# Attention scores from float16 pairs with measured scales in place of fp32r pairs, one unit in float32 rows, and one shared ring for g

## The chip, the cores and the metric

The kernel runs on one core of one Trainium2 chip. The time is the device time in microseconds of one execution; of the kernel before three executions are shown, with a median of 924.1 us. Five engines work side by side: TensorE (PE, matmuls; PEld its weight loads), VectorE (DVE), ScalarE (ACT), GpSimd (POOL) and SyncE (SP), which issues the DMAs.

## What is computed

Attention with a decay over 4 batches, 8 heads, 576 positions, 64 per head; behind it two dense blocks over the 2304 rows:

```
scores = q @ k.T / sqrt(64)                      # q, k: (4, 8, 576, 64) float32
cum    = cumsum(log(clip(f, 1e-4, 1)), axis=-1)
scores = where(causal, -1e9, scores + cum[:, :, :, None] - cum[:, :, None, :])
attn   = exp(scores - max); attn = attn / (sum(attn) + 1e-9)
x      = (attn @ v) rearranged to (2304, 512)
h      = x @ w_in; x = maximum(0.01 * h, h) @ w_out          # 512 -> 2048 -> 512
g      = x @ w_gate; out = (g * sigmoid(g) * (x @ w_val)) @ w_out2   # 512 -> 1536 -> 512
```

## The kernel before

**Units.** The work of attention and of the first dense block ("MoE" below) is cut into eight units (b, u): batch b, with u=0 for queries 0 to 319 (three tiles of 128, the first half filled) and u=1 for queries 320 to 575 (two tiles). A u=0 tile sees 128, 256 or 320 keys, a u=1 tile 448 or 576 (576 as two halves of 288). Unit (0,0) is `attention_f32`; the others go through `attention`. While one unit's attention runs, the MoE of the unit before it runs too: `along` interleaves them, so (1,0)'s scores lie beside the MoE of (0,1). `moe_h` makes g (hidden values as float16 pairs, in `g_ring`) and `moe_y` reads it into y1 in DRAM. The last part of the kernel, `gate_val` and `out_stage`, does the second dense block from y1.

**Scores.** For b = 0 a head has one float32 tile `xf` of 66 rows: 64 of k and q, and two rows that add the decay (`rd`). One float32 matmul a tile gives the scores. For b > 0 `prep_head` loads k and q doubled over 128 partitions, rounds them to fp32r (`ta`, on ScalarE), copies the rounded q to `tb`, and makes the rests by two subtractions on VectorE. Two matmuls a tile then add up: `tb` (68 rows: rounded q by rest of k, and four decay rows that `decay` left in `cum_dram`) and `ta` (128 rows). The columns of an fp32r matmul are padded to 256. `exps` then calls `exp_of`: a custom VectorE instruction scales the scores by -0.125 out of PSUM, adds the mask and takes the minimum; ScalarE does the exponential with a sum. `probs` splits the result in two float16 halves, a DMA transposes them, and `pv` multiplies with v.

**Staging.** w_gate, w_val and w_out2 come as float64 and are turned into float32 on VectorE, a piece at a time (`place`, in `gv_places`), spread over the units from (1,1) to (3,1); `prep_gv`, beside the MoE of (3,1), loads them back from DRAM and splits them.

**Order.** Every instruction is first recorded as an operation with an estimated cost; `Plan` then orders each engine's queue and SP's by a list schedule with due times, and emits it. Source order sets buffers and dependencies, and the schedule sets the order in each queue. All instructions of a unit stand under one line of the profile (415), so tiles tell them apart: `att_bytes`, `g_bytes`, `moe_bytes`, `wi_bytes`, `wo_bytes`, `stage` and `smalls` are arenas that hold many buffers; `ta` and `tb` are tiles of their own.

Of the kernel before, what the change touches and what calls it, by code (L numbers as in the profile page):

```python
# [447 lines left out]
def body(ctx, tc, qk, v, f, w_in, w_out, w_gate, w_val, w_out2, out):  # L448
# [175 lines left out]

    def decay():
# [34 lines left out]
        nc.behind = scan  # L660
        for u, (q0, nq, _) in enumerate(UNITS):
            col, _, qc, kc = COLS[u]
            for a, c, n in ((0, kc, KEYS[u]), (2, qc, nq)):
                x = csf[:, a:a + 2, col + c:col + c + n]
                nc.scalar.copy(out=x, in_=one[:, :1].unsqueeze(2).to_broadcast(x.shape))
        nc.behind = None
# [3 lines left out]
        nc.vector.memset(fr, 8.0)  # L670
        for u, (q0, nq, _) in enumerate(UNITS):
            col, wd, qc, kc = COLS[u]
            n = KEYS[u]
            ks = slice(col + kc, col + kc + n)
            qs = slice(col + qc, col + qc + nq)
            nc.vector.tensor_scalar(out=cs[:, 2, ks], in0=cum[:, :n], scalar1=-8.0, scalar2=None, op0=ALU.mult)
            nc.vector.scalar_tensor_tensor(out=cs[:, 3, ks], in0=cum[:, :n], scalar=-8.0, in1=csf[:, 2, ks],
                                           op0=ALU.mult, op1=ALU.subtract)
            nc.scalar.activation(out=cs[:, 0, qs], in_=cum[:, q0:q0 + nq], func=AF.Copy, scale=8.0)
            nc.scalar.activation(out=cs[:, 1, qs], in_=csf[:, 3, col + kc + q0:col + kc + n], func=AF.Copy, scale=-1.0)  # L680
        nc.sync.dma_start(cd, csf)
# [786 lines left out]
```

## Time and profile before

| | |
|---|---|
| median of three runs | 924.1 us (920.23 to 924.16) |
| the profiled execution | 925.66 us, of which span of the instructions 923.9 us |
| PE busy | 908.8 us, 98% of the span |
| PE weight loads | 776.7 us, 84% |
| DVE busy | 794.1 us, 86% |
| ACT busy | 676.1 us, 73% |
| POOL busy | 45.4 us, 5% |
| chain of waits that ended last | PE 58% of the span, DVE 7%, DMA 3%, ACT 3% |
| DMA queue of the kernel | 131.2 MB, 53.5% of the 16 engines' span |

Busy times are unions over the span, and matmuls overlap one another, so two starts in a row tell what a matmul costs better than its duration. A stage below is cut where a unit's MoE matmuls end: 132.6 to 187.5 us is (1,0)'s attention with the MoE of (0,1), 187.5 to 254.7 us (1,1) with the MoE of (1,0), 254.7 to 309.7 us (2,0), 309.7 to 380.2 us (2,1), 380.2 to 434.4 us (3,0), 434.4 to 499.7 us (3,1), 499.7 to 542.3 us the MoE of (3,1); then come gate_val and out_stage.

### The profile page before, as it was taken

Reading aid. Unit: us, or ns where it says so; the run is one execution under the profiler, and the core shown is the slowest. Engines: PE = TensorE matmul, PEld = TensorE weight load, DVE = VectorE, ACT = ScalarE, POOL = GpSimd, SP = SyncE. Lnnn points to the kernel's source line nnn. Section 1 sums busy time; section 2 is a strip of 40 time slices with the busy share of each in tenths; the row PEclk is TensorE's granted clock in tenths of the full one; section 3 lists DMA queues with packets and bytes.
Section 4 is the critical chain, followed back from the end, with each engine's and each line's share of the span. In section 5 each row is a group of like instructions: output and inputs, shape, how many; then the busy total and the mean of one; then the engine's idle time right before and its main releaser. Section 6 shows DMA issues by size and latency. Waiting matters only on the chain.

```text
span 923.9 us, 25387 instructions
## 1 busy us (share of the span) xinstructions
PE 908.8 (98%) x10018; PEld 776.7 (84%) x10018; DVE 794.1 (86%) x2078; ACT 676.1 (73%) x1665; POOL 45.4 (5%) x119
## 2 busy tenths in 40 slices
PE   9999999999999999899999999999999999999998
PEld 5666678877688777788778899999999999999997
DVE  7999999988899999799788999986778695968685
ACT  8886689988689887688886878774647474755553
POOL 3410000000000010000000000000000000000000
PEclk9999999999999999999999999999999999999999
DMA  7568985797999999989867452110101000100001
GB/s 229 179 202 217 271 212 115 187 248 172 259 270 259 255 263 229 298 249 254 188 147 191 140 178 96 64 59 20 37 18 31 25 25 25 37 25 2 26 6 42
DMA packets 163431, 132.81 MB, mean 144 GB/s; under 512 B 117432, under 2 KB 130752, under 8 KB 163280
## 3 DMA queue, kind: packets, MB, share of 16 engines
q1 hardware_dynamic: 163312, 131.20, 53.5%
q8 instruction: 78, 1.28, 0.6%
q14 instruction: 41, 0.34, 0.1%
HBM read 79.99 MB, written 22.83 MB: 111 GB/s over the span
## 4 chain that ended last, share of the span: by engine, by line
PE 58%; DVE 7%; DMA 3%; ACT 3%; issue 1%; POOL 0%; SPq 0%; ACTq 0%; DVEq 0%; POOLq 0%
PE bank L415 58%; DVE att_bytes L415 2%; DVE stage L415 1%; DVE wo_bytes L415 1%; ACT att_bytes L415 1%; DMA tb<-out_dram 1%; ACT moe_bytes L415 1%; DMA att_bytes<-att_bytes 1%; DVE smalls L415 1%; DVE wi_bytes L415 1%; DMA att_bytes<-in_qk_dram 1%; DMA gate_val_dram<-wo_bytes 1%; DVE g_bytes L415 1%; DVE tb L415 0%; DVE ta L415 0%
## 5 line engine op out<-in xcount | busy, mean ns | idle before, releaser
L415 PEld LDWEIGHTS <-att_bytes 128*128 128x128 f16 (+1 forms) x4062 | 233.8, 100 | 18.3 <-issue 14.7
L415 PEld LDWEIGHTS <-wi_bytes 128*128 128x128 f16 x2292 | 192.2, 98 | 42.4 <-issue 3.1
L415 PE MATMUL bank<-g_bytes,wo_bytes 128*128 128x256 f16 (+2 forms) x1472 | 209.7, 299 | 0.0
L415 PE MATMUL bank<-moe_bytes,wi_bytes 128*128 128x320 f16 (+1 forms) x1536 | 194.5, 286 | 1.5 <-ACT moe_bytes L415 1.5
L415 ACT ACTIVATE att_bytes<-att_bytes,smalls 128x320 f32<-128x320 f32 (+11 forms) x308 | 173.7, 591 | 30.1 <-DVE smalls L415 25.5
L415 PEld LDWEIGHTS <-wo_bytes 128*128 128x128 f16 x1344 | 128.1, 98 | 33.5 <-issue 1.8
L415 DVE TENSOR_TENSOR wi_bytes<-bank,wi_bytes 128x256 f32<-128x256 f32 x270 | 109.4, 418 | 45.0 <-PE bank L415 43.6
L415 PEld LDWEIGHTS <-g_bytes 128*128 128x128 f16 x1620 | 125.9, 98 | 9.0
L415 ACT ACTIVATE wi_bytes<-wi_bytes,smalls 128x256 f32<-128x256 f32 (+2 forms) x129 | 69.9, 555 | 44.9 <-DVE wi_bytes L415 42.4
L415 PE MATMUL bank<-wi_bytes,att_bytes 128*128 128x128 f16 x1680 | 98.7, 219 | 0.5 <-ACT wi_bytes L415 0.3
L415 DVE SCALAR_TENSOR_TENSOR att_bytes<-att_bytes,smalls 128x576 f16<-128x576 f32 (+5 forms) x148 | 86.8, 614 | 4.1 <-ACT att_bytes L415 3.7
L415 PE MATMUL bank<-stage,att_bytes 128*128 128x128 f16 (+1 forms) x1389 | 86.7, 221 | 0.6 <-DVE wi_bytes L415 0.6
L415 ACT COPY wi_bytes<-bank 128x256 f32<-128x256 f32 x108 | 38.4, 363 | 51.8 <-PE bank L415 47.6
L415 DVE CUSTOM_DVE_ANT_0 att_bytes<-bank,att_bytes 128x320 f32<-128x320 f32 (+5 forms) x160 | 67.7, 441 | 7.2 <-PE bank L415 7.1
L415 POOL PARTITION_ALL_REDUCE smalls<-smalls x54 | 28.2, 523 | 757.1 <-DVE smalls L415 718.3
L415 PE MATMUL bank<-att_bytes 128*64 128x256 f16 (+4 forms) x828 | 55.5, 262 | 5.5 <-DMA att_bytes<-att_bytes 5.2
L415 ACT ACTIVATE wi_bytes<-wo_bytes 128x256 bf16<-128x256 f32 x108 | 44.0, 410 | 19.2 <-DVE wo_bytes L415 19.2
L415 PE MATMUL bank<-wo_bytes,g_bytes 128*128 128x256 f16 x432 | 55.0, 273 | 0.0
L415 DVE TENSOR_TENSOR g_bytes<-moe_bytes,g_bytes 128x320 f16<-128x320 f32 (+1 forms) x80 | 44.6, 564 | 8.2 <-ACT g_bytes L415 7.8
L415 PE MATMUL bank<-tb 68*128 68x256 f32 (+3 forms) x144 | 49.9, 360 | 1.7 <-ACT att_bytes L415 1.1
L415 DVE SCALAR_TENSOR_TENSOR stage<-stage 128x512 int32<-128x512 int32 x68 | 46.5, 684 | 0.2
L415 DVE SCALAR_TENSOR_TENSOR wo_bytes<-wi_bytes,smalls 128x512 f32<-128x512 f32 x54 | 40.1, 743 | 6.3 <-ACT wi_bytes L415 6.3
(123 smaller groups left out, 1380.1 us busy)
## 6 DMA issues: line engine op xcount, KB each, us to landing
stage<-in_moe_w_out_dram SPq DMA_DIRECT2D x28, 512.0 KB
att_bytes<-in_qk_dram SPq DMA_DIRECT2D x24, 416.0 KB
stage<-in_moe_w_in_dram SPq DMA_DIRECT2D x16, 512.0 KB
att_bytes<-in_qk_dram SPq DMA_DIRECT2D x24, 320.0 KB
stage<-in_moe_w_gate_dram SPq DMA_DIRECT2D x12, 512.0 KB
stage<-in_moe_w_val_dram SPq DMA_DIRECT2D x12, 512.0 KB
stage<-gate_val_dram SPq DMA_DIRECT2D x12, 512.0 KB
ta<-y_dram SPq DMA_DIRECT2D x18, 256.0 KB
```

The lines of the kernel that those rows point to most:

```text
L415: fn(*args, **kw)
```

## The change

- Unit (1,0) takes the float32 rows that (0,1) has (`o.one`), with decay rows of its own from DRAM (`rd0`); its loads are 66 partitions in place of 128.
- For the other five units, (1,1) to (3,1), k and q are scaled by powers of two, one for each pair of heads (`sk`, `sq`), and rounded to float16 (`ta` half of a tile of `t_ring`, now four deep); the rests are float16 too (`tb` half). The scores come out scaled, and the exponent's first instruction takes its scale from memory (`nsc`). The decay rows are three float16 parts of cum, and three rows of scales as their partners, in `cum_dram`. No padding to 256 columns.
- The scales come from a scan, `prep_qk`: for each of three batches and each pair of heads it loads q and k again, three ScalarE passes with a sum of absolute values bound them, POOL reduces over partitions, VectorE makes the scales, and five kinds of small stores put the rows of scales into `cum_dram`. The scan for batch 1 stands behind the pairs of heads of (1,0), that for batch 2 in (1,1), that for batch 3 in (2,1).
- g's rings for u=0 and u=1 both start at the arena's beginning; the freed end holds the scan's buffers, the scales, and later two tiles of w_gate and w_val.

```diff
-    g_ring = [Ring([x.rearrange("p (l i q) -> p l i q", l=2, i=n) for x in a_g.cut(2 * n * u[1], F16, NF // n).bufs])
-              for n, u in zip(PER, UNITS)]
+    for n, u in zip(PER, UNITS):
+        a_g.at = 0
+        x = a_g.cut(2 * n * u[1], F16, NF // n).bufs
+        g_ring.append(Ring([y.rearrange("p (l i q) -> p l i q", l=2, i=n) for y in x]))
...
-    ta_ring = Ring([pool.tile([P, WMAX], F32R, name=f"ta{i}") for i in range(2)])
-    tb_t = [pool.tile([P, WMAX], F32R, name=f"tb{i}") for i in range(2)]
+    t_t = [pool.tile([P, WMAX], F32, name=f"tab{i}") for i in range(4)]
+    t_ring = Ring([x.bitcast(F16).rearrange("p (l n) -> p l n", l=2) for x in t_t])
...
-    xf1_ring = Ring(xf_ring.bufs + [early[:, x:x + WMAX] for x in range(n, n + 3 * WMAX, WMAX)])
+    xf1_ring = Ring(xf_ring.bufs + [t_t[3], t_t[2]])
...
+        nc.vector.tensor_scalar(out=c3[:, 0, :], in0=cum, scalar1=-8.0, scalar2=None, op0=ALU.mult)
+        nc.vector.scalar_tensor_tensor(out=low, in0=cum, scalar=-8.0, in1=c3[:, 0, :], op0=ALU.mult, op1=ALU.subtract)
+        nc.scalar.copy(out=c3[:, 1, :], in_=low)
+        nc.vector.tensor_tensor(out=c3[:, 2, :], in0=low, in1=c3[:, 1, :], op=ALU.subtract)
...
+    def prep_qk(b, hp):
+        if hp == 0:
+            amq[b] = am_r.next()
+        am = amq[b]
+        buf = qb_ring.next()
+        for x in range(2):
+            nc.sync.dma_start(buf[x * D:(x + 1) * D, :], qk[b, 2 * hp + x, :D, KEYS[0]:])
+        n0 = UNITS[0][1]
+        for i, (c, n) in enumerate(((n0, S), (0, n0), (n0 + S, S - n0))):
+            bound(am[:, i * NHP + hp:i * NHP + hp + 1], buf[:, c:c + n], buf[:, c:c + n])
+        if hp < NHP - 1:
+            return
...
+        nc.gpsimd.partition_all_reduce(al, am[:, :2 * NHP], P, ABSMAX)
...
+        for u, (q0, nq, _) in enumerate(UNITS):
+            col, wd, qc, kc = COLS[u]
+            for x, r, c, n in ((sg[:, :S], 0, kc, KEYS[u]), (sg[:, S:], 3, qc, nq)):
+                nc.sync.dma_start(cd[b * H:(b + 1) * H, r:r + 3, col + c:col + c + n],
+                                  x[:, :n].unsqueeze(1).to_broadcast((H, 3, n)))
+        qsc[b] = sk, sq, nsc
...
-        if b == 0:
+        o.one = b + u == 1
+        if o.one:
...
-        nc.scalar.copy(out=o.ta[:, :o.wd], in_=xf[:, :o.wd])
-        nc.scalar.copy(out=o.tb[:D, o.q], in_=taf[:D, o.q])
-        nc.vector.tensor_tensor(out=o.ta[D:, o.q], in0=xf[D:, o.q], in1=taf[D:, o.q], op=ALU.subtract)
-        nc.vector.tensor_tensor(out=o.tb[:D, o.k], in0=xf[:D, o.k], in1=taf[:D, o.k], op=ALU.subtract)
+        nc.scalar.activation(out=o.ta[:, o.q], in_=xf[:, o.q], func=AF.Copy, scale=sq)
+        nc.scalar.activation(out=o.ta[:, o.k], in_=xf[:, o.k], func=AF.Copy, scale=sk)
+        nc.vector.tensor_copy(out=o.tb[:D, o.q], in_=o.ta[:D, o.q])
+        nc.vector.scalar_tensor_tensor(out=o.ta[D:, o.q], in0=xf[D:, o.q], scalar=sq[D:], in1=o.ta[D:, o.q],
+                                       op0=ALU.mult, op1=ALU.subtract)
+        nc.vector.scalar_tensor_tensor(out=o.tb[:D, o.k], in0=xf[:D, o.k], scalar=sk[:D], in1=o.ta[:D, o.k],
+                                       op0=ALU.mult, op1=ALU.subtract)
...
-            parts = [(0, kw, max(kw, 256))]
+            parts = [(0, kw, kw)]
...
-            for l in range(2 if o.b else 0):
-                t, k = (o.tb, D + 4) if l == 0 else (o.ta, P)
+            for l in range(0 if o.one else 2):
+                t, k = (o.tb, D + 6) if l == 0 else (o.ta, P)
...
+               -0.125 if o.one else o.nsc)
...
+    QK_AT = {(1, 0): 1, (1, 1): 2, (2, 1): 3}
...
+            if (b, u) in QK_AT:
+                prep_qk(QK_AT[b, u], hp)
```

## Rows read from the trace of the kernel before

**Rows 1.** Windows: us of each engine busy (x instructions), granted clock, DMA share, GB/s

```profile
48.60:80.20 31.60, 31.52 (x213) 21.95 (x211) 30.96 (x85) 26.93 (x59) 3.44 (x4) 1.00 0.66 210
...
132.60:187.50 54.90, 53.78 (x530) 47.32 (x528) 51.58 (x154) 52.04 (x126) 2.66 (x5) 1.00 0.66 154
...
309.70:380.20 70.50, 68.15 (x554) 50.63 (x551) 65.08 (x188) 55.40 (x132) 3.99 (x12) 0.98 1.00 259
...
499.70:542.30 42.60, 42.60 (x398) 38.20 (x396) 40.90 (x91) 32.74 (x55) 0.50 (x2) 1.00 0.40 135
...
132.60:575.00 442.40, 434.06 (x4172) 358.37 (x4171) 403.84 (x1133) 366.99 (x858) 15.91 (x44) 1.00 0.81 210
```

**Rows 2.** Timeline of PE in (1,1): start us, us, operation, count

```profile
229.54 0.48 PE L415 MATMUL bank<-tb 68*128 68x448 f32 x1
229.86 0.37 PE L415 MATMUL bank<-ta 128*128 128x448 f32 x1
230.06 0.30 PE L415 MATMUL bank<-tb 68*128 68x288 f32 x1
...
230.61 3.43 PE L415 MATMUL bank<-g_bytes,wo_bytes 128*128 128x320 f16 x24
233.77 0.41 PE L415 MATMUL bank<-tb 68*128 68x288 f32 x1
```

**Rows 3.** Timeline of PE in (1,0)

```profile
131.65 0.52 PE L415 MATMUL bank<-tb 68*128 68x256 f32 x1
132.01 0.28 PE L415 MATMUL bank<-ta 128*128 128x256 f32 x1
...
132.68 0.50 PE L415 MATMUL bank<-moe_bytes,wi_bytes 128*128 128x256 f16 x3
```

**Rows 4.** Timeline of PE in (0,1), scores in float32 rows

```profile
69.45 1.96 PE L415 MATMUL bank<-g_bytes 66*128 66x448 f32 x6
71.25 0.98 PE L415 MATMUL bank<-moe_bytes,wi_bytes 128*128 128x320 f16 x6
```

**Rows 5.** Groups on DVE: busy us, mean ns | idle before

```profile
L415 DVE TENSOR_TENSOR tb<-att_bytes,ta 64x320 fp32r<-64x320 f32 (+1 forms) x48 | 29.3, 611 | 0.6 <-ACT ta L415 0.3
L415 DVE TENSOR_TENSOR ta<-att_bytes,ta 64x320 fp32r<-64x320 f32 (+1 forms) x48 | 21.9, 455 | 2.3 <-ACT ta L415 1.1
...
L415 DVE SCALAR_TENSOR_TENSOR att_bytes<-att_bytes,smalls 128x576 f16<-128x576 f32 x32 | 26.0, 812 | 2.3 <-ACT att_bytes L415 2.1
L415 DVE SCALAR_TENSOR_TENSOR att_bytes<-att_bytes,smalls 128x320 f16<-128x320 f32 x24 | 13.1, 544 | 0.5 <-ACT att_bytes L415 0.3
L415 DVE SCALAR_TENSOR_TENSOR att_bytes<-att_bytes,smalls 128x256 f16<-128x256 f32 x24 | 11.4, 475 | 0.0
L415 DVE CUSTOM_DVE_ANT_0 att_bytes<-bank,att_bytes,smalls 128x288 f32<-128x288 f32 x32 | 16.4, 511 | 0.5
L415 DVE CUSTOM_DVE_ANT_0 att_bytes<-bank,att_bytes 128x288 f32<-128x288 f32 x32 | 14.4, 449 | 1.1 <-PE bank L415 1.0
L415 DVE TENSOR_SCALAR wo_bytes<-wo_bytes 32x320 fp32r<-32x320 f32 x1 | 0.3, 317 | 0.3 <-ACT wo_bytes L415 0.3
L415 DVE TENSOR_TENSOR smalls<-smalls 128x1 f32<-128x1 f32 x18 | 2.6, 147 | 5.6 <-ACT wi_bytes L415 3.5 <-ACT stage L415 2.2
```

**Rows 6.** Groups on ACT

```profile
L415 ACT CAST ta<-att_bytes 128x640 fp32r<-128x640 f32 (+1 forms) x48 | 38.3, 797 | 1.9 <-DMA att_bytes<-in_qk_dram 1.2 <-PE bank L415 0.6
L415 ACT CAST tb<-ta 64x320 fp32r<-64x320 f32 (+1 forms) x48 | 20.3, 424 | 0.3
L415 ACT ACTIVATE att_bytes<-att_bytes,smalls 128x576 f16<-128x576 f32 x32 | 24.7, 772 | 8.4 <-DVE smalls L415 4.9 <-ACT tb L415 1.4 <-ACT moe_bytes L415 1.0
L415 ACT ACTIVATE att_bytes<-att_bytes,smalls 128x320 f16<-128x320 f32 x24 | 13.4, 559 | 2.3 <-DVE smalls L415 1.8 <-ACT moe_bytes L415 0.3
L415 ACT ACTIVATION_READ_ACCUMULATOR att_bytes<-att_bytes,smalls 128x1 f32 x160 | 30.3, 190 | 0.0
```

**Rows 7.** Waits, summed: us in total, times, longest us

```profile
PE bank L415 <- DMA att_bytes<-att_bytes: 5.2, 3, 2.3
```

More of the change, by code (lines that the diff above doesn't have):

```diff
@@ L620, in mms @@
         nc.done()
+    sel = early[:H, :NHP]
     def decay():
@@ L648, in decay @@
         nc.urgent = False
-        scan = next(o for o in reversed(nc.ops) if o.eng == "DVE")
         nc.filler = (banks[-1], mask[:, :P], mask[:, :4 * P])
@@ L653, in decay @@
                                 compare_op=ALU.is_ge, fill=NEG, base=0, channel_multiplier=1)
-        csf = scr[:, 3 * S:3 * S + 4 * W].rearrange("r (a s) -> r a s", a=4)
-        cs = csf.bitcast(F32R)
+        nc.gpsimd.memset(sel, 1.0)
+        for base, step in ((0, -2), (1, 2)):
+            nc.gpsimd.affine_select(out=sel, in_=sel, pattern=[[step, NHP]], compare_op=ALU.is_ge, fill=0.0,
+                                    base=base, channel_multiplier=1 if step < 0 else -1)
+        c3 = scr[:, 3 * S:].bitcast(F16)[:, :3 * S].rearrange("r (a s) -> r a s", a=3)
+        low = scr[:, 5 * S:6 * S]
         for x in ph_ring.bufs:
@@ L659, in decay @@
                 nc.gpsimd.memset(x.rearrange("p (n k) -> p n k", k=P)[:, i::9, hw:], 0.0)
[L660 to L666, printed above, removed]
         nc.scalar.copy(out=cum[:, :n0], in_=c0)
@@ L670, in decay @@
         nc.vector.memset(fr, 8.0)
+        nc.vector.tensor_scalar(out=c3[:, 0, :], in0=cum, scalar1=-8.0, scalar2=None, op0=ALU.mult)
+        nc.vector.scalar_tensor_tensor(out=low, in0=cum, scalar=-8.0, in1=c3[:, 0, :], op0=ALU.mult, op1=ALU.subtract)
+        nc.scalar.copy(out=c3[:, 1, :], in_=low)
+        nc.vector.tensor_tensor(out=c3[:, 2, :], in0=low, in1=c3[:, 1, :], op=ALU.subtract)
         for u, (q0, nq, _) in enumerate(UNITS):
             col, wd, qc, kc = COLS[u]
[L673 to L681, printed above, removed]
+            nc.sync.dma_start(cd[:, 3:, col + kc:col + kc + KEYS[u]], c3[:, :, :KEYS[u]])
+            nc.sync.dma_start(cd[:, :3, col + qc:col + qc + nq], c3[:, :, q0:q0 + nq])
+        nc.sync.dma_start(rd0, rows0[H:2 * H, :])
         nc.sync.dma_start(rd[:, 0, :S], fr[:H, :])
@@ L716, in prep_v, with cut_q @@
             vsc[b] = (sc, ix, sx)
+    at_q = 0
+    def cut_q(n, bufs=1):
+        nonlocal at_q
+        at_q += n * bufs
+        return Ring([a_q[:, at_q - (i + 1) * n:at_q - i * n] for i in range(bufs)])
+    am_r, al_r, inv_r, t_r = (cut_q(n) for n in (3 * NHP, 2 * NHP, 2 * NHP, NHP))
+    s_r, nsc_r, sig_r = cut_q(2 * NHP, 2), cut_q(NHP, 2), cut_q(NHP)
+    row_r = cut_q(1)
+    amq, qsc = {}, {}
+    def prep_qk(b, hp):
[10 more added lines that the diff above has]
+            return
+        nc.vector.tensor_tensor(out=am[:, NHP:2 * NHP], in0=am[:, NHP:2 * NHP], in1=am[:, 2 * NHP:], op=ALU.add)
+        al, inv, t, sc, nsc, sig = (r.next() for r in (al_r, inv_r, t_r, s_r, nsc_r, sig_r))
+        nc.gpsimd.partition_all_reduce(al, am[:, :2 * NHP], P, ABSMAX)
+        nc.vector.tensor_scalar(out=al.bitcast(I32), in0=al.bitcast(I32), scalar1=0x7F800000, scalar2=None,
+                                op0=ALU.bitwise_and)
+        pow2(sc, inv, al, 14)
+        sk, sq = sc[:, :NHP], sc[:, NHP:]
+        nc.vector.scalar_tensor_tensor(out=sk, in0=inv[:, NHP:], scalar=2.0 ** 15, in1=sk, op0=ALU.mult, op1=ALU.min)
+        nc.vector.tensor_tensor(out=sig, in0=sk, in1=sq, op=ALU.mult)
+        nc.vector.tensor_scalar(out=t, in0=sig, scalar1=2.0 ** -120, scalar2=-8.0, op0=ALU.max, op1=ALU.mult)
+        nc.vector.reciprocal(out=nsc, in_=t)
+        row = row_r.next()[:H, :]
+        nc.vector.tensor_tensor(out=t[:H, :], in0=sig[:H, :], in1=sel, op=ALU.mult)
+        nc.vector.tensor_reduce(out=row, in_=t[:H, :], axis=AX.X, op=ALU.max)
+        for x, n, op in ((sg[:, :S], S, ALU.subtract), (sg[:, S:], n0, ALU.add)):
+            nc.vector.tensor_scalar(out=x, in0=mask[:H, :n], scalar1=0.0, scalar2=row, op0=ALU.mult, op1=op)
+        for u, (q0, nq, _) in enumerate(UNITS):
[4 more added lines that the diff above has]
+        qsc[b] = sk, sq, nsc
```

44 lines of the change are left out of this document (27 added, 17 removed).

## The prediction

> **What bounds the kernel now.** I read four views: the windows by stage, cut where one unit's MoE matmuls end and the next one's begin, for how full each engine is; the timeline of PE, for what a score matmul costs from start to start; the groups on DVE and ACT, for durations; and the waits of PE. In the stretch from 132.6 to 575 us, which holds every unit the change touches but the first, TensorE is busy 434.1 of 442.4 us: 8.3 us idle [rows 1]. The change does not touch what PE does after 575 us. So work taken from TensorE between 132.6 and 575 us can come out of the time. The reader is to see a second thing in the same row: VectorE is busy 403.8 us of it, only 38.5 us idle, while ScalarE has 75 us idle. The stages show how far that can go: where VectorE was fullest it idled 0.6 of 31.6 us (2.0%) at 48.6 to 80.2 us, 1.7 of 42.6 (4.0%) at 499.7 to 542.3 us, and 3.3 of 54.9 (6.0%) at 132.6 to 187.5 us, where PE, DVE and ACT are all within 6% of full [rows 1]. These three shares are the yardstick below.
>
> **TensorE, the term that shrinks.** One head of a u=1 unit now issues six fp32r matmuls, 2 x (448 + 288 + 288) columns, from 229.54 to 230.61 us: 1.07 us [rows 2]. The float16 product behind it runs 24 matmuls of 320 columns from 230.61 to 233.77 us, 0.132 us each, or 0.41 ns a column. The first fp32r matmul behind float16 takes 0.32 us to the next, the second of the same size 0.20: entering fp32r costs 0.12, and each fp32r step is a little over its columns. In float16, 2048 columns are 0.84 us: 0.23 us less, for 24 heads of (1,1), (2,1), (3,1): -5.5 us. A u=0 head takes 131.65 to 132.68 us, 1.03 us for 1664 columns [rows 3], because tile 0 is padded to 256. In float16 it needs 1408 columns, 0.58 us: 0.45 less, for 16 heads of (2,0), (3,0): -7.2 us. That head comes behind float32 work, whose entry (0.36 us for 256 columns) is longer than the one behind float16, so 0.12 of the 0.45 may not be there elsewhere: -5.3 at the least. Unit (1,0) goes the other way. A head of (0,1), already in float32 rows, issues six instructions, 2048 columns, from 69.45 to 71.25 us: 0.88 ns a column, two instructions a matmul [rows 4]. So 1408 columns cost 1.24 us against 1.03: +0.2 for 8 heads, +1.7 us. The sum lies between -9.1 and -11.0; I take -10. PE's work in the stretch becomes 424 us.
>
> **VectorE, the term that grows.** Removed: the subtractions into ta and tb, 21.9 + 29.3 = 51.2 us over 48 heads [rows 5]. Added for 40 heads: two scalar_tensor_tensor with a scale from memory. The rows with the same sizes, a float16 result and such a scale took 0.544 us (320 columns), 0.475 (256) and 0.812 (576). So 16 x 2 x 0.544 + 24 x (0.475 + 0.812) = 48.3 us. That the instructions use 64 partitions is no saving: the fp32r rows on 64 partitions took as long as these do, less the scale. Further 40 copies of the rounded q, 64 x 320 or 256 in float16, which the trace does not show. Bounds: 0.147 us, a one-column instruction, and 0.317 us, 320 columns of 4 bytes by one-source tensor_scalar. I take 0.2, nearer to the fixed cost since half the bytes move: 8.0 us. The splits together are +5.1 us.
>
> The Trainium skill bears on this (VectorE: DVE Perf Modes, The perf-mode tier table): one-source copies of 16-bit data in SBUF run four results a cycle, while an instruction with two tensor sources and a float32 one stays at one a cycle, so a float16 result makes the subtractions no cheaper. The trace agrees on the second half: 64 more columns (256 to 320) cost 0.069 us in the rows above. No run here shows the copy; by that page's cycle formula it would be about 0.14 us, an estimate, and VectorE's sum 2.4 us lower.
>
> The exponent's first step (the custom instruction that reads the scores) gets its scale from memory. With one such operand the 288-column form took 0.511 us, without 0.449 [rows 5]: +0.062 for 120 instructions, +7.4 us. Lower bound nothing, upper bound twice that, if a scale costs more than a start value. The scan adds per batch some ten one-column instructions at 0.15 us and two row fills of 576 and 320 columns, 0.7 us by the 0.317 row: 2.2 us, 6.6 us for three. VectorE's sum is +19 us, to 423; bounds +10 (copies at 0.147, scales free) and +31.
>
> So the two engines want 424 and 423 us of a stretch that took 442. If nothing but PE mattered, the stretch would be 424 + 8.3 = 432.4 us, leaving VectorE 2.2% idle: only the tightest stage reached that, with work that is mostly conversion of weights. At 4.0% it is 440.5, at 6.0% 449.9. I take 437 us (3.3%): the weights' staging (gv_places) is loose filler here too, but its conversions must be done before prep_gv, whose weights gate_val needs from 542 us, so they can't be put off into the part after 575 us. **-5.4 us.**
>
> **What lies beside other work.** ScalarE: the casts of ta and tb go, 38.3 + 20.3 = 58.6 us; two scaled copies a head come, with 0.559 us for 320 columns, 0.772 for 576 and by these two 0.51 for 256, 16 x 2 x 0.559 + 24 x (0.51 + 0.772) = 48.7; and 36 scan passes, per pair of heads 0.772 + 0.559 + 0.51 with 0.19 for each read of the accumulator, 2.4 us, 28.9 us for twelve pairs [rows 6]. Net +19 of 75 us idle: hidden. Without that cover, (1,1) and (2,1) would each be up to 9.6 us longer.
>
> DMA: 24 loads of 64 rows x 1152 floats, 7.1 MB, against 1.3 MB less for (1,0). At the 259 GB/s that the stage from 309.7 us moved [rows 1], that is 22 us net of a queue busy 0.81 of the stretch. I cost it at nothing, with a rival for it. SP issues some 40 more DMAs; each head's row load from cum_dram now waits for the scan's stores, behind which later loads of that queue stand. The scan's inputs depend on nothing but two buffers, so the order can put them a unit ahead: 0; uncovered, the first scores of a unit are late by two transfers.
>
> g's shared ring: h of the next unit writes g where y of the last one reads. h's first result comes 12 matmuls of 0.132 us after its start, and y's last block reads the first groups first, so the buffers are free: 0; if not, some 2 us a unit. The fp32r ones and halves prepared in decay() go, the rest of it stays of a size, all before the stretch and beside the first unit's matmuls: 0, or a microsecond either way. Four buffers for split heads in place of two, and two fewer for float32 rows, shift loads only.
>
> **The sum.** Profiled execution 925.66 us: span 923.9, 1.8 around it. 925.66 - 5.4 = 920.3. The median of the runs shown, 924.1, lies 1.6 below that execution, so the same change gives 924.1 - 5.4 = 918.7 us: **919**.
>
> **Rivals.** (a) All of PE's saving shows: 924.1 - 10 = 914. For it: VectorE's work is loose where it stages weights. It holds if its addition is nearer +10 than +19. (b) VectorE decides, and it is slower. Place: (1,1) to (3,0), where by the terms above it gains 3 to 7 us in each stage while PE loses 2 to 4. If its idle share stays at the 6.0% of the stage where three engines balanced, the stretch is 449.9 us: +7.5, 931.6. It decides from an idle share of 4.4% up, where 422.9 / 0.956 is 442.4. Against it stand the two tighter stages. The Trainium skill (Perfetto Trace Analysis, Identifying the Most-Contended Engine) says to judge TensorE by the busy share of its weight loads, not of its matmuls. By that rule VectorE (91%) is ahead of PE (358.4 of 442.4 us, 81%) [rows 1] and should set the pace. The trace agrees only in part: an engine that sets the pace would not be idle for 38.5 us. (c) The scan's loads make DMA transpositions late: at 309.7 to 380.2 us DMA is at 1.00 and PE waited 2.3 us for one; three such waits are 5.2 us, and that stage alone has a granted clock of 0.98 [rows 1, 7]. Four more of 2.3 eat 9.2 of PE's 10 us: 923.3. (d) The float16 scores keep the entry cost, so the change does not do what it says: only the padding (16 x 256 columns x 0.41 ns, 1.7 us) goes and (1,0) takes it back; with VectorE fuller, 924 to 928.
>
> **How the numbers follow.** Forecast (co-bound, 914.5 to 924): 0.50. (a) 0.20, (b) 0.18, (c) 0.08, (d) 0.04. 0.5% is 4.6 us, about what a measurement of this kernel can tell from no change: below 919.5 and above 928.7. Faster: (a) 0.20 and 0.25 of the forecast, 0.45. Same: 0.23 of the forecast, (c) 0.07, (d) 0.03, 0.02 of (b): 0.35. Slower: 0.20. The range leaves a tenth at either end: from under (a), 911, to (b), 931.
>
> **What would show it.** Score matmuls of (1,1) on at 0.41 ns a column with no 0.32 us first step; (1,0) at 0.88 ns. VectorE's work from the start of (1,0)'s MoE to gate_val near 423 us and 96 to 97% of a stretch of 437. The scaled custom form of 288 columns at 0.51 us. PE's added idle should be behind VectorE, not DMA. Wrong if VectorE's idle share stays above 4.4%, if the scaled custom form costs nothing, or if PE waits for transpositions in (1,1) and (2,1).

## The result: 934.1 us, slower by 1.1%, and the profile after

The changed kernel took 934.14 us (median of four, 932.28 to 936.42), the kernel before 924.13 beside it: a ratio of 1.0109, interval 1.0088 to 1.013. The forecast was 919, with a range of 911 to 931: wrong in size and in sign. The execution profiled took 932.28 us, 930.6 of it span, 6.7 more than before; it was the fastest of its four, so the trace shows less than the 10.0 us between the medians.

The stages of the changed kernel, cut as before where a unit's MoE matmuls end, in the columns of [rows 1]: (0,1) with the y part of (0,0)'s MoE; a remainder before the MoE of (0,1) starts; then (1,0), (1,1), (2,0), (2,1), (3,0) and (3,1); last the whole stretch.

```profile
73.00:139.20 66.20, 59.21 (x285) 39.67 (x283) 55.10 (x153) 42.00 (x112) 2.47 (x5) 0.95 1.02 232
139.20:145.70 6.50, 5.84 (x49) 4.45 (x48) 6.50 (x34) 6.34 (x19) 0.82 (x7) 1.00 0.86 209
145.70:202.50 56.80, 54.18 (x523) 45.95 (x522) 48.72 (x148) 53.10 (x141) 2.71 (x6) 1.00 0.89 211
202.50:272.10 69.60, 66.93 (x554) 48.28 (x553) 62.13 (x186) 56.54 (x147) 2.86 (x12) 0.98 0.93 230
272.10:324.80 52.70, 52.16 (x526) 44.93 (x525) 51.87 (x158) 45.80 (x122) 3.79 (x8) 1.00 0.99 264
324.80:392.30 67.50, 66.02 (x558) 48.05 (x556) 65.16 (x192) 55.78 (x138) 2.22 (x10) 1.00 1.01 260
392.30:444.70 52.40, 51.65 (x525) 44.68 (x522) 51.99 (x168) 43.54 (x113) 1.85 (x5) 1.00 0.99 269
444.70:507.80 63.10, 63.10 (x536) 46.03 (x534) 56.51 (x155) 49.00 (x106) 0.35 (x1) 1.00 0.75 189
...
145.70:582.60 436.90, 428.74 (x4176) 348.01 (x4175) 407.88 (x1162) 364.32 (x889) 14.70 (x44) 1.00 0.84 221
```

The stage of (0,1) of the kernel before, which [rows 1] leave out, with its remainder and (1,1):

```profile
75.00:131.90 56.90, 55.35 (x315) 39.07 (x314) 54.18 (x154) 40.23 (x96) 2.07 (x9) 1.00 1.03 248
131.90:132.60 0.70, 0.70 (x7) 0.67 (x5) 0.70 (x2) 0.70 (x4) 0.00 (x0) 1.00 1.06 382
187.50:254.70 67.20, 65.58 (x549) 48.78 (x547) 58.52 (x170) 52.61 (x123) 3.98 (x13) 1.00 0.92 223
```

Laid against one another, the stretch that the forecast spoke of went from 442.4 us [rows 1] to 436.9: -5.5, where -5.4 was forecast. All the loss and more lies ahead of it. The MoE of (0,1) starts at 145.7 us in place of 132.6, 13.1 later: the stage of (0,1) took 66.2 us against 56.9, its remainder 6.5 against 0.7, and the first 73 us gave back 2.0. Inside the stretch (1,0) lost 1.9 and (1,1) 2.4; from (2,0) to (3,1) each stage was 1.8 to 3.0 us shorter (55.0 us of (2,0) became 52.7, 70.5 of (2,1) 67.5, 54.2 of (3,0) 52.4, 65.3 of (3,1) 63.1).

SP's queue of the changed kernel in the stage of (0,1) shows what is new there. Each `g_bytes<-in_qk_dram` is a load of the scan for batch 1, 288 KB:

```profile
87.23 0.34 SPq L415 DMA_DIRECT2D stage<-in_moe_w_out_dram  x1
...
88.62 1.11 SPq L415 DMA_DIRECT2D g_bytes<-in_qk_dram  x2
...
91.47 0.34 SPq L415 DMA_DIRECT2D stage<-in_moe_w_out_dram  x1
...
93.21 1.42 SPq L415 DMA_DIRECT2D g_bytes<-in_qk_dram  x2
...
113.60 1.22 SPq L415 DMA_DIRECT2D g_bytes<-in_qk_dram  x2
114.92 1.49 SPq L415 DMA_DIRECT2D stage<-in_moe_w_out_dram  x1
116.51 1.11 SPq L415 DMA_DIRECT2D g_bytes<-in_qk_dram  x2
...
125.75 0.53 SPq L415 DMA_DIRECT2D stage<-in_moe_w_out_dram  x1
126.39 3.96 SPq L415 DMA_TRANSPOSE att_bytes<-att_bytes  x1
```

All eight stand between the pieces of w_out, which (0,0)'s y needs. The DMA engines had nothing to spare there: their share was 1.03 before. In the stage's length 248 GB/s had moved 14.1 MB; now 232 GB/s moved 15.4. The 1.25 MB more are 5.0 us at the rate before, and the lower rate makes the other 4.3 of the stage's 9.3. VectorE now waits for those pieces (5.4 us against 1.6 before, by the same view), and PE for VectorE and for transpositions (for these 3.8 us against 1.3). The waits from 73 to 145.7 us, in the columns of [rows 7]:

```profile
DVE stage L415 <- DMA stage<-in_moe_w_out_dram: 5.4, 5, 1.8
...
PE bank L415 <- DMA att_bytes<-att_bytes: 3.8, 3, 2.3
```

Single heads of score matmuls came close to the forecast. PE's timeline: a (1,0) head in float32 rows (174.03), a float16 head of (2,0) (304.34), one of (1,1) (250.40).

```profile
174.03 1.36 PE L415 MATMUL bank<-att_bytes 66*128 66x128 f32 x6
175.22 4.09 PE L415 MATMUL bank<-g_bytes,wo_bytes 128*128 128x256 f16 x36
...
250.40 1.05 PE L415 MATMUL bank<-tab 70*128 70x288 f16 x6
251.28 6.68 PE L415 MATMUL bank<-g_bytes,wo_bytes 128*128 128x320 f16 x48
...
304.34 0.78 PE L415 MATMUL bank<-tab 70*128 70x256 f16 x6
304.96 1.47 PE L415 MATMUL bank<-g_bytes,wo_bytes 128*128 128x256 f16 x12
```

From start to start: 1.19 us in float32 rows (1.24 forecast), 0.88 for 2048 float16 columns (1.07 before [rows 2], 0.84 forecast), 0.62 for 1408 (1.03 before [rows 3], 0.58 forecast). The entry cost of fp32r went too. But the 1.03 us of [rows 3] was a costly head, behind float32 work. A u=0 head of the kernel before behind float16 work, the first of (2,0), takes 0.88 us:

```profile
253.81 0.38 PE L415 MATMUL bank<-tb 68*128 68x256 f32 x1
...
254.69 0.50 PE L415 MATMUL bank<-moe_bytes,wi_bytes 128*128 128x256 f16 x3
```

The 13 u=0 heads whose six matmuls stand in a row there have a median of 0.89 us. So float16 takes some 0.26 us from a u=0 head, not 0.45.

Where PE waits did change inside the stretch. First the changed kernel from 145.7 to 582.6 us, then the kernel before from 132.6 to 575 us, in the columns of [rows 7]:

```profile
PE bank L415 <- DVE smalls L415: 6.7, 10, 1.6
PE bank L415 <- DMA att_bytes<-att_bytes: 0.7, 1, 0.7
```

```profile
PE bank L415 <- DMA att_bytes<-att_bytes: 4.0, 2, 2.3
...
PE bank L415 <- DVE smalls L415: 0.5, 1, 0.5
```

VectorE's and ScalarE's new groups, which answer to [rows 5, 6]:

```profile
L415 DVE SCALAR_TENSOR_TENSOR tab<-att_bytes,g_bytes,tab 64x576 f16<-64x576 f32 x24 | 19.3, 804 | 0.0
L415 DVE SCALAR_TENSOR_TENSOR tab<-att_bytes,g_bytes,tab 64x320 f16<-64x320 f32 x32 | 17.4, 543 | 0.5
L415 DVE CUSTOM_DVE_ANT_0 att_bytes<-bank,att_bytes,g_bytes 128x288 f32<-128x288 f32 x24 | 12.1, 504 | 0.0
L415 DVE SCALAR_TENSOR_TENSOR tab<-att_bytes,g_bytes,tab 64x256 f16<-64x256 f32 x24 | 11.6, 485 | 0.7
L415 DVE COPY tab<-tab 64x256 f16<-64x256 f16 x24 | 5.2, 218 | 0.2
L415 DVE COPY tab<-tab 64x320 f16<-64x320 f16 x16 | 3.7, 229 | 0.0
...
L415 DVE CUSTOM_DVE_ANT_0 att_bytes<-bank,att_bytes 128x288 f32<-128x288 f32 x8 | 3.6, 453 | 0.0
```

The page's first lines:

```profile
PE 909.9 (98%) x10012; PEld 769.7 (83%) x10012; DVE 802.8 (86%) x2137; ACT 676.0 (73%) x1714; POOL 44.0 (5%) x125
```

The splits sum to 48.3 us as forecast, the copies to 8.9 (8.0 forecast; at 0.218 and 0.229 us each, nearer to the 0.2 taken than to the estimate of 0.14), and the scaled custom form costs 0.051 us more than the plain one (0.062 forecast). Yet VectorE is busy 8.7 us longer, not 19, and ScalarE not at all: durations of instructions back to back overlap. VectorE's groups add up to 918 us before and 942 after, in busy times of 794.1 and 802.8.

### The profile page after: what moved, and what is told of

Read it like the earlier page. It is cut to its first block, busy times and chain, and to the rows that moved or that the text cites. A ratio compares the mean times of both kernels' runs of the same rounds, so it can differ in the third digit from the quotient of the medians.

```text
span 930.6 us, 25487 instructions
## 1 busy us (share of the span) xinstructions
PE 909.9 (98%) x10012; PEld 769.7 (83%) x10012; DVE 802.8 (86%) x2137; ACT 676.0 (73%) x1714; POOL 44.0 (5%) x125
## 4 chain that ended last, share of the span: by engine, by line
PE 58%; DVE 10%; ACT 2%; DMA 2%; issue 1%; ACTq 0%
PE bank L415 58%; DVE att_bytes L415 4%; DVE stage L415 2%; DVE tab L415 2%; ACT att_bytes L415 1%; DVE smalls L415 1%; DMA att_bytes<-att_bytes 1%; DVE g_bytes L415 1%; DMA stage<-in_moe_w_val_dram 1%; DMA att_bytes<-in_qk_dram 1%; DVE wo_bytes L415 1%; DVE wi_bytes L415 1%; ACT tab L415 0%; DVE moe_bytes L415 0%; ACT wi_bytes L415 0%
## 5 line engine op out<-in xcount | busy, mean ns | idle before, releaser
L415 PE MATMUL bank<-g_bytes,wo_bytes 128*128 128x256 f16 (+2 forms) x1472 | 213.9, 300 | 1.6 <-DVE wo_bytes L415 1.6
L415 ACT ACTIVATE att_bytes<-att_bytes,smalls 128x576 f32<-128x576 f32 (+11 forms) x308 | 173.3, 590 | 37.1 <-DVE smalls L415 25.7
L415 PE MATMUL bank<-moe_bytes,wi_bytes 128*128 128x320 f16 (+1 forms) x1536 | 191.1, 286 | 0.0
L415 PEld LDWEIGHTS <-wo_bytes 128*128 128x128 f16 x1344 | 130.7, 98 | 34.0 <-issue 0.5
L415 DVE SCALAR_TENSOR_TENSOR att_bytes<-att_bytes,smalls 128x448 f16<-128x448 f32 (+5 forms) x148 | 86.2, 614 | 8.3 <-ACT att_bytes L415 8.2
L415 PE MATMUL bank<-att_bytes 128*64 128x256 f16 (+6 forms) x852 | 62.3, 266 | 5.9 <-DMA att_bytes<-att_bytes 4.6
L415 PE MATMUL bank<-tab 70*128 70x288 f16 (+14 forms) x288 | 56.3, 312 | 8.3 <-DVE smalls L415 7.4
L415 ACT ACTIVATE tab<-att_bytes,g_bytes 128x576 f16<-128x576 f32 (+2 forms) x80 | 46.5, 602 | 7.9 <-DMA att_bytes<-in_qk_dram 7.6
L415 DVE SCALAR_TENSOR_TENSOR tab<-att_bytes,g_bytes,tab 64x576 f16<-64x576 f32 (+2 forms) x80 | 48.3, 604 | 1.3
L415 DVE CUSTOM_DVE_ANT_0 att_bytes<-bank,att_bytes,g_bytes 128x288 f32<-128x288 f32 (+4 forms) x96 | 47.8, 522 | 1.0 <-PE bank L415 0.7
```

Of the source, the lines that this page charges most:

```text
L415: fn(*args, **kw)
```

## The theories

1: the scan's loads for batch 1 enter a stage whose DMA is full; the change is sound and the scan's place is the cost. 2: (1,0) in float32 rows costs more than its matmuls show. 3: g's shared ring makes h of one unit wait for y of the last. 4: the scans cost through their passes, by loading ScalarE and VectorE and by giving their scales late. 5: the planner orders the whole program anew at each edit, and the order is worth what is measured, luck and not cause. The expectations below call 2 to 4 rivals.

## Experiments on the scan

Each ratio is against the kernel before on the same chip, where its median was 923.0 to 923.9 us. Two experiments that are set against one another may come from two chips, so a difference of about 1 us between them says nothing.

**a1_late_scan**: the scan's loads for batch 1 held behind (1,0)'s first scores.

```diff
+        if b == 1:
+            if hp == 0:
+                hold[0] = next(o for o in reversed(nc.ops) if o.eng == "PE")
+            nc.behind = hold[0]
```

> The changed kernel, with the loads of batch 1's scan held behind the first scores of (1,0); the same work later. Theory 1 (in the stage of (0,1) DMA is full with w_out's pieces, and eight scan loads of 288 KB delay those pieces and the transpositions): most of the 9 us that this stage lost and of the 6 us behind it come back, 920 to 926 us. Rival 2 (the float32 rows of (1,0) and their fewer buffers): no change, 934. Rival 3 (h of (0,1) waits for g's shared ring): 934. Rival 4 (the passes on ScalarE and VectorE): 930 to 934, as the passes only move.

930.17 us, ratio 1.0068 [1.0045, 1.0091]: theory 1 missed by 4 us, and the time lies in the range of the passes (theory 4). The stage of (0,1) is whole again, and a later one pays. Its windows:

```profile
75.00:132.00 57.00, 56.55 (x309) 39.88 (x308) 53.95 (x157) 38.07 (x92) 2.90 (x10) 1.00 0.98 233
...
190.00:260.00 70.00, 64.97 (x502) 46.11 (x501) 60.78 (x184) 61.40 (x163) 3.99 (x10) 0.95 1.08 233
```

PE is idle 0.45 of the first 57 us, and the MoE of (0,1) starts at 134.1 us in place of 145.7. But PE is idle 5.0 of the 70 us around (1,1), with DMA at 1.08: 2.4 behind ScalarE and 2.3 behind a transposition, and the clock is 0.95. Held back, the loads give that stage its 11.6 us and the kernel only 4.0; this run does not tell whether loads or passes cost the rest.

**a2_scan1_const** and **a3_scan1_no_load**: batch 1 with constants in place of the scan's loads and passes; and with its passes, but on a buffer filled once. The reduction, the arithmetic of the scales and their stores stay in both.

```diff
# a2
+        if b == 1:
+            for i in range(3):
+                nc.vector.memset(am[:, i * NHP + hp:i * NHP + hp + 1], 200.0)
# a3
+        if b > 1:
             for x in range(2):
                 nc.sync.dma_start(buf[x * D:(x + 1) * D, :], qk[b, 2 * hp + x, :D, KEYS[0]:])
+        elif hp < 2:
+            nc.gpsimd.memset(buf, 0.5)
```

> The changed kernel without batch 1's scan: no loads and no passes for that batch, its scales from a constant (the values of its scales are left out, all matmuls stay). Theory 1: 917 to 924 us, the whole loss of (0,1) back and (1,0) lighter. Rivals 2 and 3: 930 to 934. Rival 4: as theory 1; the next kernel tells them apart.

> The changed kernel with batch 1's passes but without its loads: the twelve passes read a constant buffer (batch 1's scales are left out as such). Theory 1 (the loads): 918 to 925 us, close to the kernel without the scan. Rival 4 (the passes): 930 to 934. Rivals 2 and 3: 930 to 934.

a2: 921.18 us, 0.9976 [0.9959, 0.9993]. a3: 925.46, 1.002 [1.0001, 1.0039]. The scan for batch 1 is worth 13.0 us (934.1 to 921.2); of these its loads are 8.7 (934.1 to 925.5), its passes and late scales 4.3. a3 lies half a microsecond above what theory 1 expected, and 4.5 under what theory 4 did.

**b2_no_scan**: constants in place of the loads and passes of all three batches; the reductions, the arithmetic and the stores stay.

```diff
-            bound(am[:, i * NHP + hp:i * NHP + hp + 1], buf[:, c:c + n], buf[:, c:c + n])
+        for i in range(3):
+            nc.vector.memset(am[:, i * NHP + hp:i * NHP + hp + 1], 200.0)
```

> The changed kernel with no scan at all: the scales of all three batches from a constant (left out: every load and pass of the scan). It shows what float16 pairs, float32 rows and the ring bring by themselves. If the scans of batches 2 and 3 are hidden, it is the time of the kernel without batch 1's scan, 919 to 923 us; if they cost, 911 to 917. If the shared ring costs 5 us or more by itself, it stays above 917.

914.37 us, 0.99 [0.9884, 0.9917], 9.3 under the 923.7 of before. The loads and passes of the scans take 19.8 (934.1 to 914.4). The 9.3 are near the 10 that the forecast took from PE, but they are not all PE's work. From the start of the MoE of (0,1) to that of (3,1), before and in b2:

```profile
132.60:499.70 367.10, 359.97 (x3224) 289.18 (x3223) 333.64 (x972) 307.56 (x736) 14.75 (x41) 1.00 0.89 224
```

```profile
133.30:490.40 357.10, 353.26 (x3217) 278.25 (x3217) 339.04 (x1022) 295.30 (x719) 14.99 (x41) 1.00 0.90 228
```

Of the 10.0 us between them 6.7 are PE's busy time, 1.3 of that a stretch at the lower clock that the kernel before had there (last section); the other 3.3 are idle time.

**c2_passes23**: the passes for batches 2 and 3 kept, all loads left out, batch 1 constant as in a2.

```diff
-        for x in range(2):
-            nc.sync.dma_start(buf[x * D:(x + 1) * D, :], qk[b, 2 * hp + x, :D, KEYS[0]:])
...
+            if b == 2 and hp < 2:
+                nc.gpsimd.memset(buf, 0.5)
```

> The changed kernel with constant scales for batch 1 (no pass, no load) and, for batches 2 and 3, the passes over a buffer that is filled once, without the loads of q and k; so it leaves out all loads of the scan. Without any scan 914.4 us were measured, with the scans of batches 2 and 3 whole 921.2. If those 7 us are loads that crowd the DMA queues: 914 to 917. If they are VectorE's passes and the arithmetic of the scales: 919 to 922.

919.0 us, 0.9934 [0.9912, 0.9956]: from 914.4 the passes and what hangs on them add 4.6 us, and the loads (to a2's 921.2) 2.2. By the ratios, each against its own chip, the same two are 3.1 and 3.9. So both cost something, and which costs more is not shown.

**v1_early_scan**: batch 1's scan placed between (0,0)'s heads, where DMA has room, on buffers of its own, over 832 columns in place of 1152. **v2_scans_ahead**: besides, batch 2's scan one unit sooner and batch 3's two.

```diff
+            for x in range(2):
+                nc.urgent = True
+                nc.sync.dma_start(buf[x * D:(x + 1) * D, :], qk[b, 2 * hp + x, :D, KEYS[0] + n0:])
+                nc.urgent = False
+                nc.ops[-1].behind = gate[hp]
...
# v2
-    QK_AT = {(1, 0): 1, (1, 1): 2, (2, 1): 3}
+    QK_AT = {(1, 0): 2, (1, 1): 3}
```

> A repair: batch 1's scan early, in two of the split heads' buffers, its loads ahead of the others from the heads of (0,0) on, where DMA is busy 0.66, and without the 320 query columns that (1,1) does not use. Theory 1: the 9 us of (0,1) come back, 921 to 926 us, and the wait for w_out's pieces is that of the kernel before. If the passes on ScalarE matter more (rival 4), 926 to 932.

> The changed kernel with batch 1's scan early (before the stage of (0,1), over 832 columns of keys) and the scans of batches 2 and 3 one pair of units sooner. The version with only batch 1's scan early gave 922.5 us. If the scans of batches 2 and 3 cost by coming late to their units: 916 to 920. If they cost by their passes on VectorE or by DMA wherever they stand: 921 to 925, and more if the stages of (1,0) and (1,1) have less room than the later ones.

v1: 922.49 us, 0.9994 [0.9976, 1.0013]. v2: 921.62, 0.9974 [0.9956, 0.9993]. Windows of v1, the first 75 us:

```profile
0.00:75.00 75.00, 72.47 (x420) 46.55 (x421) 66.52 (x216) 63.82 (x193) 19.59 (x53) 1.00 0.82 219
```

DMA's share there is 0.82, against 0.67 in the changed kernel, and PE's busy time falls from 73.3 to 72.5. v1 takes back 11.6 of the 13.0 us that a2 takes back by leaving the scan out. But it is a repair and no second proof of theory 1: its stage of (0,1) is not free of scan loads. The order puts all eight of batch 2 and two of batch 3 there (98.2 to 137.8 us on SP's queue). DMA's share from 82.6 to 141.1 us is 1.05, VectorE's wait for w_out's pieces is 3.0 us from 75 to 150 us (1.6 before), and the MoE of (0,1) starts at 141.1 us, 4.6 sooner than in the changed kernel and 8.4 later than before. The rest comes behind: from there to the MoE of (3,1) v1 took 354.5 us and the changed kernel 362.1. Putting the others sooner adds 0.9, no more than chance, as expected if the scans cost wherever they stand. v2 computes everything and is 12.5 us ahead of the changed kernel, 2.2 ahead of the one before, in one order.

## Experiments on the ring, the rows and the order

**a4_ring_only**: the kernel before with the shared ring alone (first block below; what lies in the freed end moves with it, two tiles of w_gate and w_val among it). **a4_ring_order2**: the same with other random numbers in the planner's trials. **b1_ring_rows**: besides the ring, (1,0) in float32 rows (second block), the other units in fp32r pairs.

```diff
+    for n, u in zip(PER, UNITS):
+        a_g.at = 0
+        x = a_g.cut(2 * n * u[1], F16, NF // n).bufs
+        g_ring.append(Ring([y.rearrange("p (l i q) -> p l i q", l=2, i=n) for y in x]))
# b1 besides
-        if b == 0:
+        o.one = b + u == 1
+        if o.one:
```

> The kernel before with one part of the change: g's rings of both units start at the same place. Theory 1: within 3 us of before, 921 to 927 us. Rival 3: h of (0,1) starts late by 6 us or more, 930 to 936 us.

> The kernel before with the shared ring alone, in another order of the planner's. Theory 3 (the ring costs 6 us or more by what it forbids): 929 to 933 again. Theory 5 (the order's luck, some 2 us either way around 925): 922 to 927.

> The kernel before with the shared ring and with (1,0) in float32 rows, on five buffers; no float16, no scan. The prediction's term: 1.7 us over the shared ring alone, so 930 to 934 if the ring costs 7, 924 to 928 if it costs nothing. Rival 2 (the float32 rows cost far more than their matmuls): 936 or above.

a4: 930.13 us, 1.0075 [1.0055, 1.0094]; in the other order 928.77, 1.0064 [1.0039, 1.0089]. b1: 932.57, 1.0098 [1.0076, 1.012]. So the ring, costed at nothing, seemed to be 5 to 7 us, and the rows 2.4 on top (1.7 forecast), or 3.8 against a4's other order, which ran on b1's chip. But the trace of a4 shows no h waiting for a y: ScalarE's casts into g idled 1.2 us in all. What else moves with the ring is `o2_t`, a buffer for w_out2 at the end: before it lies under the short unit's ring, and so may not be filled until that ring's last use.

**c1_ring_o2_under**: a4 with `o2_t` put back under the ring. **c5_o2_free**: the converse, two rings as before and `o2_t` moved out from under. Neither changes an operation.

```diff
# c1
+    us_0 = a_g.cut(2 * NA * P, F16, 4).bufs
     sum_t = a_g.cut(NA * P, F32).rearrange("p (a n) -> p a n", a=NA)
     a_g.at -= 2 * NA * P * 2
     o2_t = a_g.cut(4 * DH, F32)
+    us_0 = [x.rearrange("p (l a n) -> p l a n", l=2, a=NA)
+            for x in us_0 + a_g.cut(2 * NA * P, F16, 2).bufs + a_a.cut(2 * NA * P, F16, 1).bufs]
# c5
     sum_t = a_g.cut(NA * P, F32).rearrange("p (a n) -> p a n", a=NA)
     a_g.at -= 2 * NA * P * 2
     o2_t = a_g.cut(4 * DH, F32)
+    us_0 = [x.rearrange("p (l a n) -> p l a n", l=2, a=NA)
+            for t, n in ((a_g, 6), (a_a, 1)) for x in t.cut(2 * NA * P, F16, n).bufs]
```

> The kernel before with g's ring shared by both units, and o2_t put back under the ring's space of the short unit, as it lies in the kernel before. If the shared ring alone costs 5 to 7 us because o2_t is no longer held back by that ring, so that the last steps of y(3,1) and gate_val mix, this gives back to about the kernel before: 923 to 925 us. If the cost lies in the ring itself, one set of five buffers where two sets stood: 928 to 931.

> The kernel before with its two rings, and only o2_t and sum_t moved out from under the short unit's ring. If o2_t's freedom is the cost that the shared ring brought: 928 to 931 us. If the ring itself is: 922 to 926, the kernel before within the two microseconds that other orders make.

c1: 922.56 us, 0.9985 [0.9965, 1.0004]. c5: 932.57, 1.0077 [1.005, 1.0104]. The ring itself costs nothing, and the buffer's place 7.6 to 8.7 us: by these two runs a clear finding. It did not carry over.

**d1_after_o2_under** and **v3_ahead_o2_under**: the same edit in the changed kernel, and in v2.

> The changed kernel with o2_t alone moved back under the short unit's ring. In the kernel before, this place took back all that the shared ring cost (930.1 to 922.6 us). If it does the same here, 925 to 929 us where the changed kernel had 934. If the cost of the place only showed in the kernel before because its order was a lucky one: 932 to 936.

> The version with all three scans sooner (921.6 us) and with o2_t under the ring. If the two repairs add up: 913 to 917. If they take back the same waits: 919 to 923.

d1: 937.52 us, 1.0146 [1.0131, 1.0161], 3.4 more than the changed kernel. v3: 929.14, 1.0046 [1.0029, 1.0062], 7.5 more than v2. The edit that took 7.6 us from one kernel added 3.4 and 7.5 to two others; both times lie above all that was expected. So `o2_t`'s place is not a fixed cost. With fp32r pairs it went one way each time: under the ring 922.6 (c1) and 924.1 to 927.0 us (three orders of the kernel before, the others below), free 928.8, 930.1 (a4) and 932.6 (c5). In the two kernels with float16 it went the other way, by 3.4 us, about what an order alone makes (below), and by 7.5. Why is not shown. The place changes what follows what at the end; the planner works out due times backward from the end (`backward`), and SP's queues differ from 13.7 us on (a4 and c1), 20.8 (v2 and v3) and 62.3 (the changed kernel and d1). The loss is not at the end: from the MoE of (0,1) to that of (3,1) a4 took 371.1 us and c1 364.9, and behind it 425.4 and 424.6.

How much an order alone is worth: **before_order2** and **a4_ring_order2** with other random numbers, **before_order3**, **after_order2** and **after_order3** with the planner's third, second and third best order.

```diff
-            r = random.Random(k)
+            r = random.Random(k + 100)
# the others
+            found.setdefault(end, (end, order, [(op.start, op.end) for op in self.ops]))
...
+        best = found[sorted(found)[2]]
```

> The kernel before, unchanged but for the random numbers by which the planner picks one of its 80 orders: another order, nearly as good by its own measure. If the 7 us of the shared ring alone are the ring's (theory 3), another order without that part stays within 2 us of 923. If they are the order's luck (theory 5: any edit draws a new order, and orders of equal rank differ by several us on the chip), it lies anywhere from 918 to 932.

> As the one above, a third order (the planner's third best). Theory 3: within 2 us of 923. Theory 5: anywhere from 918 to 932, and not the same as the two others.

> The changed kernel, the planner's second best order. Theory 1 (the loads of batch 1's scan cost 9 us in any order, since DMA is full there): 930 to 938. Theory 5: 922 to 940.

> The changed kernel, the planner's third best order. Theory 1: 930 to 938. Theory 5: 922 to 940, and not the same as the two others.

The kernel before in other orders: 924.48 us (1.0017 [1.0002, 1.0032]) and 926.98 (1.0038 [1.0022, 1.0053]). The changed kernel: 935.96 (1.013 [1.0099, 1.016]) and 932.9 (1.0104 [1.0066, 1.0142]). With d1 the changed kernel has four orders, at 932.9 to 937.5, 935.1 in the mean. The arithmetic of before has seven (before three times, c5, a4 twice, c1), at 922.6 to 932.6, 927.1 in the mean. The two groups only touch, so theory 5 does not explain the loss. Kernels that differ in the order alone lie closer: 924.1 to 927.0 (before), 928.8 to 930.1 (a4), 932.9 to 936.0 (the changed kernel). So an order alone made up to 3.1 us here; an edit that moves one buffer, and the order with it, made up to 8.7.

What stays in all orders of the changed kernel is the hole in the stage of (0,1), the idle time of PE there. From 75 to 150 us, the changed kernel in its own order and its second best, then b2 and a3:

```profile
75.00:150.00 75.00, 67.35 (x358) 46.59 (x356) 63.69 (x191) 50.64 (x137) 3.29 (x11) 0.95 1.00 226
```

```profile
75.00:150.00 75.00, 64.18 (x322) 44.14 (x320) 61.76 (x183) 48.24 (x132) 2.93 (x11) 0.94 0.98 221
```

```profile
75.00:150.00 75.00, 73.76 (x482) 54.92 (x481) 71.44 (x254) 55.38 (x135) 3.33 (x12) 1.00 0.87 203
```

```profile
75.00:150.00 75.00, 73.40 (x475) 54.34 (x473) 70.56 (x219) 62.57 (x169) 5.65 (x13) 1.00 0.99 230
```

With the loads PE is idle 7.6 and 10.8 of the 75 us and gets through 358 and 322 of its recorded matmuls (368 and 328 in the third order and in d1); without them it is idle 1.2 and 1.6 and gets through 482 and 475. Even a3, which keeps the passes, has no hole. The start of the MoE of (0,1) sums it up. With the eight loads in the stage before it, it is at 144.3 to 148.8 us, in four orders. In the five kernels with the same ring, rows and float16 and without those loads (a1, a2, a3, b2, c2) it is at 133.1 to 135.3; in the three orders of the kernel before at 130.6 to 132.7. In v2, with four loads of batch 2 there, it is at 137.7, in v3 with six at 141.0. One run does not fit: b1 has no scan, and starts at 139.8, with PE idle 4.2 us from 75 to 150 us. So a hole of half that size can come without loads, and what made it there is open.

In the other orders PE waits for transpositions each time (6.3, 3.9 and 4.9 us from 75 to 150 us in the second best, the third best and d1; 1.3 in the kernel before). VectorE's wait for the pieces of w_out is 5.1, 3.9 and only 0.8. So it is the late transpositions that go with the hole in every order.

## Why the prediction was wrong

**The step that failed** is "I cost it at nothing", of the scan's loads, with the sentence behind it that the order "can put them a unit ahead: 0". It set the bytes against DMA's share in the stretch from 132.6 us on, 0.81 [rows 1]. But the eight loads of batch 1 that the order puts a unit ahead land before that stretch, in the stage of (0,1), whose share was 1.03. That window was in reach and was not read. Measured, those loads are worth 8.7 us (a3), and the scan for batch 1 as a whole 13.0 (a2). That the loads make the hole is shown: it is there in four orders and gone in five kernels without them. Its size in the kernel's time, some 9 us, is known to the scatter of the orders. That the place alone is the cost, as theory 1 has it, is not shown: a later place gave back 4.0 us (a1), and an earlier one 11.6 with the other scans moved as well (v1). Rival (c), scan loads that make transpositions late, had the mechanism and the wrong place (the stretch, where PE's waits for them fell from 4.0 to 0.7 us).

**The scans' passes**, ScalarE's 28.9 us and VectorE's 6.6, were taken as hidden or as part of VectorE's sum. They measured 4.3 us for batch 1 and 3.1 to 4.6 for the other two, each little more than an order alone made, so theory 4 is likely and not proved singly. All three scans together, 19.8 us, are more than any order made.

**TensorE's term** had the right sign and was too large. The u=1 heads gave 0.19 us each (0.23 forecast), the u=0 heads some 0.26 (0.45), and a head in float32 rows cost some 0.3 more (0.2): -4.6, -4.2 and +2.4, together -6.4 where -10 was taken and -9.1 was the bound. The error is in [rows 3]: one head was read, and it was a costly one. All score matmuls of the program together, from each start to the next without idle time, say the same: 74.4 us before, 69.0 in the changed kernel, 67.6 in b2. So b2's 914.4, half a microsecond from rival (a), is in part luck: a third of what it gained in the stretch was idle time.

**VectorE as a second bound** was half right. The addition was summed from durations, +19, and came to 4.1 us of busy time in the stretch (403.8 to 407.9), since instructions back to back overlap. VectorE's idle share there is 6.6%, above the 4.4% that the prediction named as a sign that it is wrong. The floor of 2 to 6% for idle shares was wrong too: in (2,0) VectorE was idle 0.83 of 52.7 us (1.6%), in (3,0) 0.41 of 52.4 (0.8%), and both stages still gave back 2.3 and 1.8 us. But PE's waits did move as foretold: 6.7 us behind VectorE in place of 0.5, and 0.7 behind transpositions in place of 4.0; 5.1 of the 6.7 are in (1,0) and (1,1), the two stages that lost time. That the stretch came out at 436.9 us against a forecast of 437 is an accident: PE's busy time in it fell by 5.3 us, not 10, and its idle time stayed (8.3 and 8.2 us) where the forecast had it grow by 4.6. The Trainium skill (Perfetto Trace Analysis, Identifying the Most-Contended Engine) would have VectorE set the pace. In b2 VectorE was busy 5.4 us longer than before in a stretch 10.0 us shorter, so the traces speak against it here.

**g's shared ring at nothing** holds for the ring itself: c1 has it at 922.6 us. With the buffer that it frees it cost 5 to 7 us in the kernel before, in two orders (a4). What it costs in the changed kernel no run shows, and which kernels the buffer's place helps stays open: it was not seen which of the many moved waits make it up. **Float32 rows**: +1.7 forecast, 2.4 or 3.8 measured (b1 against the two orders of a4), inside the scatter. The parts do not add up: from b1, with ring and rows, to b2, with float16 besides, the time falls by 18.2 us, far more than the scores took from PE. What the forecast had no term for is this: each edit draws a new order, which moved this kernel by up to 3 us where nothing else changed.

## What to carry to other kernels

New loads are priced at the place where the queue will issue them, not where they are used: read DMA's share stage by stage, and from the first stage in which their inputs are free. A pass over the inputs that makes a cheaper arithmetic possible is part of the arithmetic's price; measure the kernel once with the pass's result as a constant, and the two come apart. Where a planner orders everything, give each variant two or three orders before a difference of some microseconds is called an effect, and try an edit in more than one kernel: `o2_t`'s place looked proved by an edit and its converse, and changed sign in the next two.

## What the runs showed of the hardware

Some short idles of TensorE were followed by a stretch at the lower clock. In the changed kernel PE waited 2.29 us for a transposition, went on at 132.54, and from 133.6 us ran at 1.2 GHz for 3.4 us, with work all the time. Its windows there:

```profile
133.10:133.50 0.40, 0.40 (x12) 0.40 (x9) 0.11 (x1) 0.40 (x2) 0.00 (x0) 1.00 0.60 192
133.60:137.00 3.40, 3.40 (x19) 2.55 (x15) 2.88 (x12) 2.51 (x8) 0.46 (x1) 0.51 0.90 219
137.10:137.50 0.40, 0.40 (x4) 0.31 (x3) 0.00 (x0) 0.40 (x3) 0.00 (x0) 1.00 0.65 66
```

The same came in the kernel before behind an idle of 2.35 us. Its timeline of PE:

```profile
374.68 1.79 PE L415 MATMUL bank<-att_bytes 128*64 128x256 f16 x29 [2.35 <-DMA att_bytes<-att_bytes]
376.40 3.19 PE L415 MATMUL bank<-g_bytes,wo_bytes 128*128 128x320 f16 x12
379.32 0.39 PE L415 MATMUL bank<-tb 68*128 68x256 f32 x1
```

Twelve matmuls of 320 columns took 2.92 us there, 0.243 each where 0.132 is usual [rows 2]: 1.3 us more, which no view counts as a wait. With two further stretches of this kind, from 99.4 and 239.5 us, the changed kernel's clock is 0.95 and 0.98 in the stages of (0,1) and (1,1). Each of the two followed two idles close together behind VectorE, of 1.01 and 0.28 us and of 1.61 and 0.87 us. The length of one idle does not foretell it. c5 was idle longer, and its granted clock stayed at 1.00 from 379.3 to 386 us:

```profile
379.29 1.56 PE L415 MATMUL bank<-att_bytes 128*64 128x256 f16 x29 [2.85 <-DMA att_bytes<-att_bytes]
```
